# A fused attention and spectral kernel on one core: a room for each transposed tile, full-width score units, and a new order

## The chip, the cores and the metric

The kernel runs on one core of a Trainium2 chip. A core has five engines that run their own instruction streams: TensorE (PE) for matrix products, VectorE (DVE), ScalarE (ACT) and GpSimd (POOL) for elementwise work, and SyncE (SP), which here only issues transfers. Matrix products read SBUF and write PSUM, eight banks of 128 partitions x 2 KB. Engines wait for each other on semaphores. The metric is device microseconds of one execution. Before the change three runs took 235.37 us in the median (235.24 to 236.7).

## The reference

Two branches over the same 2048 x 640 input are mixed by a gate. Branch A is attention of 32 heads of 20 columns in four segments of 512 tokens: causal softmax inside a segment, and a linear memory over the segments before.

```
for s in range(4):
    p = softmax(q[s] @ k[s].T * scale + causal mask)
    a_dot = p @ v[s]
    a_mem = (phi(q[s]) @ M) / (phi(q[s]) @ z + 1e-6)     # phi(t) = t+1 if t>0 else exp(t)
    o[s] = g * a_mem + (1 - g) * a_dot                   # g = sigmoid(beta), by head
    M += phi(k[s]).T @ v[s];  z += phi(k[s]).sum()
a = o @ wo
b = irfft2(rfft2(x) * (w_r + 1j * w_i))
out = gate * a + (1 - gate) * b                          # gate = sigmoid(x . gate_w), by token
```

## The kernel before

**One recorded list, one order.** `Kern.record` (L866) does not issue anything: it records operations in a list, each with the buffers that it reads and writes. `Sched.schedule` (L117) then takes the constant `ORDER`, a list of some 2,300 numbers; each names an operation and the engine that does it, where two can. This order was made beforehand and is written into the file. So each engine's instruction stream is fixed, and each stream runs in order. `Sched.emit` puts in the semaphore waits. A transfer waits in SP's stream like an instruction in another, so what stands behind it on SP waits too.

**Modes of PE.** Most products use the full array (mode 0). Scores contract over 20 rows and run in four row tiles (mode 1). Products with few output partitions run in four column tiles of 32 (mode 2); a product of 128 output columns may be split into four of them when the neighbours in the order are column-tiled. `FLAT` in `finish_tile` names one output tile that is kept in mode 0.

**Attention.** Per segment the projections of queries and keys (`proj`) go to PSUM, to SBUF, to a scratch tensor in DRAM, and back as padded tiles `qkp` (L602). Eight groups of four heads follow, two to a pair. `qk_unit` (L1326) makes one unit of scores into the four banks of the pool "qk", which holds one unit at a time, and one exponential (L1367, in the last segment L1358) takes them to `ex` in SBUF. Keys come in pieces of kinds a, b and c. Kinds a and b are a full unit of 2048 columns for one group; kind c has 512 columns per group. `wide(s)` says whether kind c is done for four groups at once, a full unit for two pairs (segments 1 and 2), or for two, half a unit for each pair (segments 0 and 3). `masks` (L1373) lets POOL zero the upper triangle of the diagonal blocks and copy half blocks into place (L1404). In segments 0 to 2 the product with the values is made transposed (`pv_flipped`), stored to a scratch tensor and loaded again as `oU` for the output projection; in segment 3 it is made directly (`pv_group`) and transposed on PE at the end (`last_transposes`).

**The last segment's own layout.** Segment 3 keeps its exponentials with a pitch of 1280 columns per head, in three rooms of 5120 columns which lie across the rooms of the segments before. Therefore exponentials of its first three groups are recorded behind the last readers of several older rooms (`ex3`). Kind b there takes two exponentials (1280 and 768 columns) per group, and kind c two of 512 per pair.

**Memory.** `mem_read` reads the memory of the segments before; for segments 1 and 2 its result goes to a scratch tensor `o_scr`, and `finish_tile` (L1629) loads it back transposed as `mT`, 128 tokens a time, and adds it to `oU` (L1657). There are eight such loads (L600) and three rooms for them, taken in turn; these rooms lie in the space that the transform's tables use before. Each load also waits for its room.

**Transform.** `fft` makes column and row transforms as matrix products (`F1`, `D`, `T`), the product with the filter on DVE (L1560), and the inverse (`Tb`, `Db`) into `G`, which `finish_tile` reads. The operands `eo` of the last step lie on `xT[0]`.

**Output.** `finish_tile` adds the gated transform (`Fb`) and the output projection (`oproj`, helper L565 for products that were split into column tiles, L567 for others) in PSUM; ACT or DVE evicts (`ot`) and SP stores.

Of the kernel before, what the change touches and what calls it, by code (L numbers as in the profile page):

```python
# [7 lines left out]
ACT = mybir.ActivationFunctionType  # L8
# [502 lines left out]
class Kern:  # L511
# [84 lines left out]
    def dma(self, dst, src, nbytes, r, w, prio, tr=False, name="", after=(), queue="sp"):  # L596
# [1133 lines left out]
```

## Time and profile before

| what | value |
|---|---|
| median of three runs | 235.37 us (235.24 to 236.7) |
| the profiled execution, its own time | 237.45 us |
| its span, first to last instruction | 235.7 us |
| PE, DVE, ACT, POOL busy | 95%, 83%, 82%, 64% |
| granted TensorE clock | 0.993 |
| matmuls in the trace | 4377 of 4391 |
| transfers | 42.19 MB, mean 179 GB/s |

The tables of the profile group instructions by line, engine and operands: out<-in with shapes, the count, busy time and mean duration in ns of one, then the idle time of that engine in front of them and what ended it. "PEld" is the loading of weights, which overlaps matmuls. A row of the timeline has start, length, engine and group. Most matmuls are recorded by one helper line (L567) and evictions by another (L577 on ACT, L579 on DVE), so the tile names tell them apart. Since matmuls are pipelined, the distance from one start to the next tells more than the duration of one.

### The profile page before, as it was taken

What the parts mean: (1) busy time and instruction counts of PE and PEld (TensorE: products, weight loads), DVE (VectorE), ACT (ScalarE), POOL (GpSimd) and SP (SyncE); (2) the same over time, 40 slices, a digit from 0 to 9 for tenths busy, and PEclk for the clock granted to TensorE, in tenths of its full rate; (3) what the DMA queues carried; (4) which work ended last, traced back from release to release, by engine and by line L of the source; (5) the groups of instructions that cost most, each with busy time, mean ns of one, the idle gap of its engine ahead of it and who ended that gap; (6) DMA issues with size and microseconds to landing.
All of it is one profiled execution on the core that took longest, in us unless ns stands there. A gap on an engine that the chain in (4) does not pass through costs nothing.

```text
span 235.7 us, 10361 instructions
## 1 busy us (share of the span) xinstructions
PE 224.1 (95%) x4377; PEld 141.7 (60%) x4391; DVE 195.1 (83%) x497; ACT 193.1 (82%) x221; POOL 151.0 (64%) x299
## 2 busy tenths in 40 slices
PE   6799999999999999999999999999999999999993
PEld 2477577666546666555556645656544467667793
DVE  0169998799999996899999898999899984856563
ACT  2069997989899999999999889999999789787720
POOL 8233128445766886566786558677879687797810
PEclk9799999999999999999999999999999999999999
DMA  6999959999989356978654686376969687463124
GB/s 150 280 340 245 238 146 167 175 212 200 192 234 219 85 164 192 215 161 208 181 157 128 196 239 204 106 214 210 215 168 275 207 147 127 114 107 109 37 83 113
DMA packets 59266, 42.19 MB, mean 179 GB/s; under 512 B 30228, under 2 KB 55380, under 8 KB 59220
## 3 DMA queue, kind: packets, MB, share of 16 engines
q1 hardware_dynamic: 58180, 40.96, 73.8%
q8 instruction: 34, 0.56, 1.0%
q10 hardware_dynamic: 1040, 0.57, 0.9%
q14 instruction: 12, 0.10, 0.1%
HBM read 23.32 MB, written 12.30 MB: 151 GB/s over the span
## 4 chain that ended last, share of the span: by engine, by line
PE 71%; DVE 17%; DMA 7%; issue 2%; ACT 1%; SPq 1%; DVEq 0%
PE psum L567 63%; PE psum L565 8%; DVE Pt L1560 3%; DMA qkp<-qk_scr 3%; DMA xT<-in_A_x_dram 2%; DMA Wt<-in_B_w_r_dram 2%; DVE va L1183 2%; DVE G L1606 1%; DVE ub L579 1%; DVE Cp L579 1%; DVE mem L1228 1%; DVE dn L1223 1%; DVE mem L1225 1%; DVE qu L579 1%; ACT ex L1358 1%
## 5 line engine op out<-in xcount | busy, mean ns | idle before, releaser
L1404 POOL TENSOR_SCALAR_AFFINE_SELECT ex<-ex 128x256 bf16<-128x256 bf16 (+3 forms) x224 | 104.7, 487 | 40.1 <-ACT ex L1367 6.2
L1367 ACT ACTIVATE ex<-psum 128x2048 bf16<-128x2048 f32 (+1 forms) x56 | 101.7, 1816 | 7.9 <-PE psum L567 6.3
L1358 ACT ACTIVATE ex<-psum 128x1280 bf16<-128x1280 f32 (+3 forms) x32 | 36.2, 1130 | 7.4 <-PE psum L567 6.7
L567 PE MATMUL psum<-qkp 20*64 20x64 bf16 (+5 forms) x1280 | 32.1, 270 | 1.6 <-ACT ex L1367 1.0
L567 PE MATMUL psum<-xT,wk 128*128 128x256 bf16 (+1 forms) x280 | 33.0, 286 | 0.2
L567 PE MATMUL psum<-xT,wq 128*128 128x512 bf16 (+1 forms) x121 | 29.1, 422 | 2.9 <-DMA xT<-in_A_x_dram 2.1
L567 PE MATMUL psum<-wv,xT 128*32 128x321 bf16 (+3 forms) x385 | 26.8, 301 | 0.0
L1560 DVE TENSOR_TENSOR Pt<-psum,Wt 128x642 bf16<-128x642 f32 x32 | 25.5, 821 | 0.4
L567 PEld LDWEIGHTS psum<-xT,wk 128*128 128x128 bf16 (+1 forms) x280 | 20.4, 102 | 7.7 <-issue 3.0
L567 PEld LDWEIGHTS psum<-qkp 20*64 20x64 bf16 x1280 | 13.5, 103 | 18.0 <-ACT ex L1367 10.3
L973 POOL TENSOR_TENSOR xsb<-xf 128x320 bf16<-128x320 bf16 (+2 forms) x11 | 8.1, 743 | 19.8 <-DVE xf L968 10.5
L565 PE MATMUL psum<-wo,oU 128*32 128x320 bf16 x460 | 19.9, 300 | 0.0
L567 PE MATMUL psum<-big,Cp 128*128 128x321 bf16 (+1 forms) x96 | 19.1, 303 | 0.2
L567 PE MATMUL psum<-big,Ac 128*128 128x160 bf16 (+2 forms) x96 | 18.1, 257 | 0.3 <-DVE va L1183 0.2
L579 DVE CAST ot<-psum 128x320 bf16<-128x320 f32 x21 | 9.9, 489 | 9.3 <-PE psum L565 6.9
L567 PEld LDWEIGHTS psum<-wv,xT 128*32 128x32 bf16 (+1 forms) x385 | 13.4, 96 | 7.0 <-issue 1.8
L567 PE MATMUL psum<-ex,va 128*32 128x64 bf16 (+3 forms) x576 | 17.2, 256 | 0.3 <-ACT qu L577 0.3
L1183 DVE TENSOR_TENSOR va<-psum,ebx 128x320 bf16<-128x320 f32 x32 | 15.3, 485 | 2.0 <-PE psum L567 0.7
L567 PE MATMUL psum<-tt,Yt 128*128 128x256 bf16 (+1 forms) x96 | 16.2, 275 | 0.4 <-ACT qu L577 0.2
L1606 DVE TENSOR_TENSOR G<-eo,psum 128x320 bf16<-128x320 f32 x32 | 14.7, 478 | 2.1 <-PE psum L567 1.9
L567 PEld LDWEIGHTS psum<-ex,va 128*32 128x32 bf16 x576 | 10.9, 96 | 8.6 <-issue 1.3
L1140 ACT ACTIVATE et<-qu 128x512 bf16<-128x512 bf16 x25 | 15.6, 626 | 0.0
(103 smaller groups left out, 405.2 us busy)
## 6 DMA issues: line engine op xcount, KB each, us to landing
qkp<-qk_scr SPq DMA_DIRECT2D x28, 160.0 KB
tt<-tab_tt SPq DMA_DIRECT2D x8, 512.0 KB, 4.2
qk_scr<-qu SPq DMA_DIRECT2D x12, 256.0 KB, 3.8
u_scr<-ub SPq DMA_DIRECT2D x12, 256.0 KB, 3.6
xsb<-in_A_x_dram SPq DMA_DIRECT2D x8, 320.0 KB, 5.7
oU<-u_scr SPq DMA_DIRECT2D x15, 128.0 KB, 4.9
out_dram<-ot SPq DMA_DIRECT2D x12, 160.0 KB
Wt<-in_B_w_r_dram SPq DMA_DIRECT2D x16, 80.2 KB, 3.6
```

The lines of the kernel that those rows point to most:

```text
L565: h = e.matmul(dst, wt, r_, start=st, stop=sp_, **{**kw, "tile_position": (0, q), "skip_group_check": True})
L567: h = e.matmul(o_, l_, r_, start=st, stop=sp_, **kw)
L579: alts["dve"] = (lambda e: e.tensor_copy(dst(), src()), 67 + 1.04 * n, 68.0)
L973: self.either(lambda e, dst=dst, src=src, d0=d0, n=n, op=op: e.tensor_tensor(xs.ap(o + dst, [D, 2], [1, n]), xf.ap(src + d0, [321, 2], [1, ...
L1140: self.one("act", lambda e: e.activation(et.ap(0, [1, L]), qsl(), ACT.Exp), L, [qb], [b("et", pi_)], late, fix=95, name="phi_exp")
L1183: self.one("dve", lambda e: e.tensor_tensor(va.ap(i * H * VW + h0 * VW, [VW, nh], [1, DH]), self.ps(bank, 0, [DH, nh], [1, DH]), self.ebx. ...
L1223: self.one("dve", lambda e: e.reciprocal(dn.ap(16, [1, 16]), dn.ap(0, [1, 16])), 16, [db], [rb], prio, fix=145, name="mem_rec")
L1358: self.one("act", lambda e, d=d, q=q: e.activation(self.ex.ap(*d), self.ps(bank, *q), ACT.Exp, scale=SC), (2048, (1280, 768)[x], 512)[kind ...
L1367: self.one("act", lambda e, d=d, q=q: e.activation(self.ex.ap(*d), self.ps(bank, *q), ACT.Exp, scale=SC), 2048 if kind < 2 else 512 * n, [ ...
L1404: self.one("pool", lambda e: e.affine_select(self.ex.ap(*d, p0=p0, np_=np_), self.ex.ap(*q, p0=p0, np_=np_), [[0, 4], [1, n]], ALU.is_ge, ...
L1560: self.one("dve", lambda e, ri=ri, Pt=Pt, Wt=Wt, wo_=wo_, bank=bank: e.tensor_tensor(Pt.ap(ri * 322, [644, 2], [1, KD]), self.ps(bank, 0, ...
L1606: self.one("dve", lambda e, q=q, n2=n2, bank=bank, eo=eo: e.tensor_tensor(self.G.ap(n2 * D + 639 * q, [1 - 2 * q, 320]), eo.ap(q, [1, 320] ...
```

## The change

Three things are changed by hand and one follows from them.

1. **Rooms for the memory tiles.** Each of the eight `mT` tiles has a room of its own. Three of segment 2 keep the old rooms; the fourth lies on `qu[0]`, the four of segment 1 on `xT[0]`, which is free after the projections of segment 2. So that `xT[0]` is free, `eo` moves to `phk`, and one slice of the output weights from `phk` to `et`.
2. **Full-width score units.** Segment 3 uses the layout of the other segments (pitch 1088, kind c apart), so kind b is one exponential of 2048 columns. Kind c is done for four groups at once in segment 3 and in the second half of segment 0. The half blocks that segment 3 needs side by side are copied by the masks into a new room `X2COL`, on `Macc` (free after the last memory update); kind c of groups 4 to 7 lies on `ub`.
3. **Recording.** `fft_out` is split off `fft` and recorded after all segments. `FLAT` names another tile.
4. **A new `ORDER`** for all engines: 100 lines of numbers, nearly all different. Where an operation can go to two engines the choice may differ as well.

```
-        self.mT = [TL(f"mT{i}", [P, 5 * P]) for i in range(3)]
+        self.mT = {(2, i + 1): TL(f"mT{i}", [P, 5 * P]) for i in range(3)}
...
-        self.eo = [T(f"eo{i}", [P, 322], F32, at=self.xT[0].off + i * 1344) for i in range(3)]
+        self.mT.update({(1, i): T(f"mTx{i}", [P, 5 * P], at=self.xT[0].off + i * 1280) for i in range(4)})
+        self.mT[2, 0] = T("mTq", [P, 5 * P], at=self.qu[0].off)
...
+        self.eo = [T(f"eo{i}", [P, 322], F32, at=self.phk[0].off + i * 1344) for i in range(3)]
...
-            if self.wide(s):
+            if self.wide(s, pr):
...
-    def wide(self, s):
-        return s in (1, 2)
+    def wide(self, s, pr):
+        return s > 0 or pr > 1
...
     def exo(self, s, g):
-        return g % 3 * 5120 if s == 3 else self.EBASE + ((s * 8 + g) % 3) * 4 * self.EPITCH
+        return self.EBASE + ((s * 8 + g) % 3) * 4 * self.EPITCH
...
-        if s == 3:
-            step = self.exo(s, g + 1) - e0 if kind == 2 else 0
-            if kind == 0:
-                outs = [((e0, [1280, 4], [1, 512]), (0, [512, 4], [1, 512]))]
-            elif kind == 1:
-                outs = [((e0 + 576, [1280, 4], [1, 320]), (0, [512, 4], [1, 320])), ((e0 + 960, [1280, 4], [1, 192]), (320, [512, 4], [1, 192]))]
-            else:
-                outs = [((e0 + 896 + x * step, [1280, 4], [320, 2], [1, 64]), (x * 128, [512, 4], [64, 2], [1, 64])) for x in range(2)]
...
+        if kind == 2:
+            d, q = (self.exc(s, g), [128, 4], [512, n], [1, 128]), (0, [512, 4], [128, n], [1, 128])
         else:
...
+            d, q = (e0 + 576 * kind, [self.EPITCH, 4], [1, 512]), (0, [512, 4], [1, 512])
...
+                self.mask(s, g, P, (x0 + 64, cp), (e0 + 896, ep), 64, ("b0",), ("x2",), prio, 64)
+        elif s == 3:
+            self.mask(s, g, P, (x0, cp), (c0, cp), 64, ("c0",), ("x2c",), prio, 0)
+            self.mask(s, g, 64, (c0, cp), None, 64, (), ("c0",), prio, 0, 64)
+            self.mask(s, g, 64, (c0, cp), None, P, (), ("c0",), prio, -64)
...
-    FLAT = ((1, 0, 1),)
+    FLAT = ((1, 2, 0),)
...
-                self.mtc = getattr(self, "mtc", -1) + 1
-                k3 = self.mtc % 3
-                mT, mb = self.mT[k3], b("mT", k3)
+                mT, mb = self.mT[s, a], b("mT", s, a)
+                if s == 1:
+                    home = [b("xT", 0, c) for c in range(5)]
+                else:
+                    home = self.after_mid(("mT", a)) if a else [b("qu", 0, x) for x in range(2)]
```

On PE the same 4391 matmuls stand in a new order. ACT has 213 instructions for 230, DVE 499 for 497, POOL 303 and SP 239 on both sides.

More of the change, by code (lines that the diff above doesn't have):

```diff
@@ L808, in alloc @@
         self.va = [T(f"va{i}", [P, 4 * H * VW + 16]) for i in range(2)]
-        self.wo = [T(f"wo{c}", [P, D], at=self.pkn.off + 1280 * c if c < 4 else self.phk[0].off) for c in range(5)]
+        self.wo = [T(f"wo{c}", [P, D], at=self.pkn.off + 1280 * c if c < 4 else self.et[0].off) for c in range(5)]
         self.oU += [T("oU1", [P, 5 * L], at=self.phq.off), T("oU2", [P, 5 * L], at=self.va[0].off)]
         self.NEX = 3
-        self.ex = T("ex", [P, self.ONCOL + 4 * D])
+        self.ex = T("ex", [P, self.X2COL + 3 * 4 * P])
         self.cur = self.ex.off + 2 * self.ONCOL
@@ L822, in alloc @@
         self.Macc = T("Macc", [P, 880], F32)
+        assert self.ub[0].off == self.ex.off + 2 * self.UBCOL and self.Macc.off == self.ex.off + 2 * self.X2COL
         self.Mz = [T(f"Mz{i}", [P, 880]) for i in range(2)]
@@ L926, in late_weights @@
         for c in range(5):
-            home = [b("pkn", t) for t in range(5)] if c < 4 else [b("phk", k, x * L) for k in range(2) for x in range(2)]
+            home = [b("pkn", t) for t in range(5)] if c < 4 else [b("et", k) for k in range(2)]
             self.dma(lambda c=c: self.wo[c].ap(0, [1, D]), lambda c=c: dap(self.wo_d, 4 * c * D, [DH * D, H], [D, 4], [1, D]),
@@ L1300 @@
     ONCOL = MBASE + 512
+    UBCOL = ONCOL + 2 * 4 * D
+    X2COL = UBCOL + 4 * L + 4 * P
     def exb(self, s, g, k):
-        if s == 3:
-            return self.b("ex3", g % 3, k)
+        if s == 3 and (k[0] == "x" or k == "c0" and g > 3):
+            return self.b("ex3", g % 3 if k[0] == "x" else g, k)
         if k == "c0":
@@ L1307, in exb @@
         return self.b("ex", (s * 8 + g) % 3, k)
[L1309 to L1312 removed]
     def exo(self, s, g):
[L1315 removed]
+        return self.EBASE + ((s * 8 + g) % 3) * 4 * self.EPITCH
     def exc(self, s, g):
[L1318 removed]
+        return 512 * g if g < 4 else (self.UBCOL if s == 3 else self.MBASE + 768) + 512 * (g - 4)
     def exm(self, s, g):
@@ L1323, in exall @@
     def exall(self, s, g):
-        return [self.exb(s, g, k) for k in ("a0", "b0", "c0", "m1", "m3") + ("b1",) * (s == 3)]
+        return [self.exb(s, g, k) for k in ("a0", "b0", "c0", "m1") + (("m3",) if s < 3 else ("x2", "x2c"))]
     def qk_unit(self, s, pr, u, unit):
@@ L1348, in qk_unit @@
         e0, n = self.exo(s, g), len(gps)
-        if s == 3:
-            step = self.exo(s, g + 1) - e0 if kind == 2 else 0
-            if kind == 0:
-                outs = [((e0, [1280, 4], [1, 512]), (0, [512, 4], [1, 512]))]
-            elif kind == 1:
-                outs = [((e0 + 576, [1280, 4], [1, 320]), (0, [512, 4], [1, 320])), ((e0 + 960, [1280, 4], [1, 192]), (320, [512, 4], [1, 192]))]
-            else:
-                outs = [((e0 + 896 + x * step, [1280, 4], [320, 2], [1, 64]), (x * 128, [512, 4], [64, 2], [1, 64])) for x in range(2)]
-            for x, (d, q) in enumerate(outs):
-                self.one("act", lambda e, d=d, q=q: e.activation(self.ex.ap(*d), self.ps(bank, *q), ACT.Exp, scale=SC), (2048, (1280, 768)[x], 512)[kind], [bank],
-                         [self.exb(s, 2 * pr + (x if kind == 2 else gp), ks + str(x * (kind == 1))) for gp in gps], prio - self.QK_LEAD, name="exp" + str(x)[x == 0:],
-                         after=[q for gp in gps if 2 * pr + gp < 3 for q in self.ex3(2 * pr + gp)])
-        else:
-            if kind == 2:
-                d, q = (self.exc(s, g), [128, 4], [512, n], [1, 128]), (0, [512, 4], [128, n], [1, 128])
-            else:
-                d, q = (e0 + 576 * kind, [self.EPITCH, 4], [1, 512]), (0, [512, 4], [1, 512])
-            home = [b("xf", k) for k in range(3)] if s == 0 and kind == 2 and pr > 1 else []
-            self.one("act", lambda e, d=d, q=q: e.activation(self.ex.ap(*d), self.ps(bank, *q), ACT.Exp, scale=SC), 2048 if kind < 2 else 512 * n, [bank],
-                     [self.exb(s, 2 * pr + gp, ks + "0") for gp in gps], prio - self.QK_LEAD, name="exp", after=home)
@@ new lines, in qk_unit @@
+        if kind == 2:
+            d, q = (self.exc(s, g), [128, 4], [512, n], [1, 128]), (0, [512, 4], [128, n], [1, 128])
+        else:
+            d, q = (e0 + 576 * kind, [self.EPITCH, 4], [1, 512]), (0, [512, 4], [1, 512])
+        home = [b("xf", k) for k in range(3)] if s == 0 and kind == 2 and pr > 1 else []
+        if s == 3 and kind == 2 and pr > 1:
+            home = [b("ub", k, x) for k in range(2) for x in range(2)]
+        self.one("act", lambda e, d=d, q=q: e.activation(self.ex.ap(*d), self.ps(bank, *q), ACT.Exp, scale=SC), 2048 if kind < 2 else 512 * n, [bank],
+                 [self.exb(s, 2 * pr + gp, ks + "0") for gp in gps], prio - self.QK_LEAD, name="exp", after=home)
@@ L1405, in mask @@
             self.ex.ap(*d, p0=p0, np_=np_), self.ex.ap(*q, p0=p0, np_=np_), [[0, 4], [1, n]], ALU.is_ge, 0.0, base=base, channel_multiplier=-1), 4 * n,
-            [self.exb(s, g, k) for k in rk], [self.exb(s, g, k) for k in wk], prio, per=0.793, fix=218, name="mask")
+            [self.exb(s, g, k) for k in rk], [self.exb(s, g, k) for k in wk], prio, per=0.793, fix=218, name="mask",
+                 after=[self.b("Macc", t) for t in range(5)] * (wk[0][0] == "x"))
         self.Sc.ops[-1].part = p0 > 0
@@ L1435, in pv_group @@
                         items.append((th, 22))
-                self.mms(items, [self.exb(s, g, k) for k in (("a0",), ("a0", "b0", "m1"), ("a0", "b0", "b1", "c0", "m1"), ("a0", "b0", "b1", "c0", "m1", "m3"))[i]] + [b("va", s % 2, jj) for jj in range(i + 1)] + [bank], [],
+                self.mms(items, [self.exb(s, g, k) for k in (("a0",), ("a0", "b0", "m1"), ("a0", "b0", "m1", "x2", "x2c"), ("a0", "b0", "c0", "m1"))[i]] + [b("va", s % 2, jj) for jj in range(i + 1)] + [bank], [],
                          prio, name="pv")
@@ L1585, in fft, with fft_out @@
                            after=[b("xsb", q) for q in range(8)])
+    def fft_out(self):
+        b = self.b
+        tot = 10.3 + 65.7 + 51.3
+        tf = lambda c: self.F_START + (self.F_END - self.F_START) * c / tot
+        big = self.big
+        acb = [b("Ac", c, nb) for c in range(5) for nb in range(4)]
         cpb = [b("Cp", g, c0) for g in range(16) for c0 in (0, 2)]
@@ L1602, in fft @@
                     self.Sc.op(self.copy_alts(lambda eo=eo: eo.ap(0, [1, KD]), lambda bank=bank: self.ps(bank, 0, [1, KD]), KD),
-                               r=[bank], w=[eb], prio=prio, name="ev_Db", after=[b("xT", 0, c) for c in range(5)])
+                               r=[bank], w=[eb], prio=prio, name="ev_Db", after=[b("phk", x, y * L) for x in range(2) for y in range(2)])
                     continue
```

45 lines of the change are left out of this document (16 added, 29 removed), and 188 rows, old and new, of the table ORDER.

## The prediction

> **What bounds the kernel now.** I read the busy shares of the whole span first:
>
> ```profile
> PE 224.1 (95%) x4377; PEld 141.7 (60%) x4391; DVE 195.1 (83%) x497; ACT 193.1 (82%) x221; POOL 151.0 (64%) x299
> ```
>
> That line is one average. The second view is the busy time in three stretches: the middle (attention over segments 0 to 2 beside the transform), the tail (the last segment beside the output projections), and the finish.
>
> ```profile
> 45.00:185.00 140.00, 135.84 (x2454) 81.23 (x2463) 130.93 (x333) 130.33 (x138) 99.92 (x207) 1.00 0.79 192
> 185.00:229.00 44.00, 43.89 (x1274) 31.26 (x1270) 30.52 (x79) 32.84 (x39) 30.93 (x57) 1.00 0.51 109
> 229.00:236.00 7.00, 2.98 (x88) 2.62 (x80) 2.77 (x6) 0.44 (x1) 0.00 (x0) 1.00 0.36 98
> ```
>
> The columns are length, PE, PE's weight loads, DVE, ACT, POOL, clock, DMA. In the tail PE is busy 43.89 of 44.00 us, while ACT and DVE have 11 and 13 us free. So there only less PE work shortens the time. In the middle PE is not busy for 140.00 - 135.84 = 4.16 us, ACT (130.33) and DVE (130.93) are busy 93% too, and the three wait for each other in turn. The third view, the waits of the weight loads in the same 140 us, says on whom:
>
> ```profile
> PEld psum L567 <- ACT ex L1367: 10.1, 35, 0.9
> ```
>
> Weight loads waited 35 times for an exponential: all four score banks are one room, so the next score unit starts only when the exponential has read the last one. Most of these 10.1 us pass beside matmuls still running. The order of the first 30 us hardly changes. Neither does the finish: behind the last matmuls
>
> ```profile
> 230.31 1.67 PE L567 MATMUL psum<-wo,oTl 128*32 128x320 bf16 x44
> ```
>
> come a copy and the store on both sides, some 3.7 us to the span's 235.7. What can move is the middle and the tail.
>
> **The change, part by part.**
>
> **Changes of tile mode on PE.** The number of matmuls is 4391 on both sides, of the same shapes. What differs is how often PE goes between full-array, row-tiled (scores) and column-tiled work. In the program's order I count 211 such changes before and 204 after: 167 and 166 up to the first output projection, 44 and 38 behind it. What one costs, from start to start:
>
> ```profile
> 138.76 0.30 PE L567 MATMUL psum<-wv,xT 128*128 128x320 bf16 x1
> 138.99 0.73 PE L567 MATMUL psum<-ex,va 128*32 128x512 bf16 x24
> 139.54 1.02 PE L567 MATMUL psum<-wv,xT 128*32 128x320 bf16 x24
> 140.49 0.43 PE L567 MATMUL psum<-qkp 20*64 20x512 bf16 x12
> 140.97 0.31 PE L567 MATMUL psum<-wv,xT 128*128 128x321 bf16 x1
> 141.11 0.30 PE L567 MATMUL psum<-big,Ac 128*128 128x321 bf16 x1
> 219.54 0.31 PE L565 MATMUL psum<-wo,oU 128*32 128x320 bf16 x4
> 219.68 0.31 PE L567 MATMUL psum<-G,fbg 128*32 128x320 bf16 x4
> ```
>
> Without a change a 321-column matmul takes 141.11 - 140.97 = 0.14 us of PE, and four column-tiled ones of 320 take 219.68 - 219.54 = 0.14. With one, the 320 columns at 138.76 take 0.23: 0.09 for the change. The 24 tiled ones at 139.54 take 0.95 where six fours need 0.84: 0.11. Seven fewer at 0.11 are **-0.8 us**; six of them lie in the tail, where nothing can absorb the gain. Ends: 0.09 each gives -0.6, and double that, -1.3, if those that vanish also hid a wait.
>
> **Cover of the waits.** This is the large term, and an estimate. For each group of matmuls that reads what ACT, DVE or POOL made, I went back in the program's order to the matmul that this came from, and set the PE work that stands in between (columns at 0.14 us for 321, plus the changes of mode) against the durations of the instructions on the way. For a score unit the way is the exponential of the unit before:
>
> ```profile
> L1367 ACT ACTIVATE ex<-psum 128x2048 bf16<-128x2048 f32 x52 | 97.6, 1877 | 7.4 <-PE psum L567 6.0
> L1367 ACT ACTIVATE ex<-psum 128x1024 bf16<-128x1024 f32 x4 | 4.1, 1023 | 0.5 <-PE psum L567 0.3
> L1358 ACT ACTIVATE ex<-psum 128x2048 bf16<-128x2048 f32 x8 | 15.0, 1877 | 3.8 <-PE psum L567 3.8
> L1358 ACT ACTIVATE ex<-psum 128x1280 bf16<-128x1280 f32 x8 | 9.9, 1237 | 2.1 <-PE psum L567 2.0
> L1358 ACT ACTIVATE ex<-psum 128x768 bf16<-128x768 f32 x8 | 6.5, 810 | 0.3
> L1358 ACT ACTIVATE ex<-psum 128x512 bf16<-128x512 f32 x8 | 4.8, 597 | 1.2 <-PE psum L567 0.9
> L1560 DVE TENSOR_TENSOR Pt<-psum,Wt 128x642 bf16<-128x642 f32 x32 | 25.5, 821 | 0.4
> ```
>
> So fewer than about 2.1 us of PE work between two score units (1.877 and a hand-over) means a wait that no luck removes; behind the product with the filter (L1560) it is 0.82 and a hand-over. Before, 26 groups of the middle lack 4.8 us in all, 10 of them score units; in the tail none lacks any. That agrees with the 4.16 and 0.11 us in which PE is not busy, and so I trust the count. After, 18 groups of the middle lack 2.3 us (8 are score units), and 2 of the tail lack 0.56 (a score unit and one that follows the transform's last sums). The difference is -2.5 + 0.56 = -1.9 us. The count knows nothing of ACT and DVE being held up by other work in their own queues, and both are 93% busy; so I take **-1.4**, with 0 and -1.9 as the ends.
>
> **The exponentials themselves.** Before they take 52 x 1.877 + 4 x 1.023 + 8 x (1.877 + 1.237 + 0.810 + 0.597) = 137.9 us; after, 71 of 2048 and 2 of 1024 columns take 135.3: 2.6 us and 17 instructions less, and 73 score units for 76. Of the 2.6 nearly all is in the last segment, the tail, where ACT has 11 us to spare: its worth is in the cover above, and **0** by itself.
>
> **Copies that change engines.** Net, two 512-wide evictions go from ACT to DVE; from POOL to DVE go one sum with the memory tile, one normalisation, one gate table and one sum of the last segment, and one transform sum goes to POOL.
>
> ```profile
> L579 DVE CAST qu<-psum 128x512 bf16<-128x512 f32 x16 | 11.0, 685 | 1.9 <-PE psum L567 1.4 <-ACT et L1140 0.3
> L1657 DVE TENSOR_TENSOR oU<-oU,mT 128x640 bf16<-128x640 bf16 x6 | 3.2, 550 | 0.5 <-DMA mT<-o_scr 0.5
> L1649 DVE TENSOR_TENSOR oU<-oU,r 128x512 bf16<-128x512 bf16 x10 | 3.7, 418 | 0.0
> L1090 DVE TENSOR_TENSOR fbg<-fcat,gbc 128x512 bf16<-128x512 bf16 x2 | 1.4, 683 | 0.0
> L1450 DVE TENSOR_TENSOR on<-on,mem 128x320 bf16<-128x320 bf16 x4 | 1.6, 426 | 0.0
> L1565 DVE TENSOR_TENSOR Yt<-Pt 128x321 bf16<-128x321 bf16 x17 | 5.2, 322 | 0.0
> ```
>
> DVE gets 2 x 0.685 + 0.550 + 0.418 + 0.683 + 0.426 - 0.322 = 3.1 us more. The four from POOL are work for the output and lie mostly in the tail, where DVE has 13 us free: **0**. The two evictions (1.4 us) can fall in the middle; without cover they cost +1.4, and as they free ACT as much, as little as -1.4. I take 0.
>
> **Masks.** Eight of 128x256 go and eight of 64x256 come:
>
> ```profile
> L1404 POOL TENSOR_SCALAR_AFFINE_SELECT ex<-ex 128x256 bf16<-128x256 bf16 x104 | 42.7, 421 | 16.2 <-ACT ex L1367 2.7 <-DVE oU L1649 2.1 <-DVE Ac L579 1.8
> L1404 POOL TENSOR_SCALAR_AFFINE_SELECT ex<-ex 64x256 bf16<-64x256 bf16 x48 | 19.9, 416 | 12.3 <-DVE phk L1153 5.1 <-PE psum L567 2.0 <-DVE phq L1153 1.7
> ```
>
> At 421 and 416 ns these are equal: 0. The layout of the last segment is now that of the others, so its first units no longer wait for several old rooms at once; that is in the cover too.
>
> **The rooms for the memory tiles.** The only wait on such a load stands in the L1657 row above: 0.5 us of DVE, in a tail where PE is never idle. So having them early is worth **0**, 0.5 at most. But the loads are on SP's queue:
>
> ```profile
> L600 SPq DMA_TRANSPOSE mT<-o_scr x8: 1227/1293/1911, 167.8 to 206.9; - x8
> DMA to landing us min/median/max: 4.5/4.5/4.5
> ```
>
> Before, three of the eight stand ahead of the last load of padded queries and keys on that queue; after, seven do, four more. Each holds the queue for 1.29 us, and the score units wait for what stands behind it. I take 0, as the projections run far ahead of their scores in both orders; the other end is 4 x 1.29 = +5.2.
>
> **Sum.** -0.8 - 1.4 = -2.2 us. The profiled execution took 237.45 us (span 235.7), 2.1 more than the median of the runs, 235.37. From 237.45 the sum gives 235.25; applied to the median, **233.2 us**, 0.9% less. A measurement of this kernel can tell about 1%, 2.4 us, from no change.
>
> **The rivals.** *More than the count says.* The 10.1 us of weight loads behind exponentials are mostly hidden below "busy", as matmuls are pipelined. If the new order takes the share from them that it takes from my count (2.5 of 4.8, a half), that is -5.0, with the modes and the tail's 0.56 about -5.3: 230.1 us. For it: the weight loads are busy 58% of the middle and 71% of the tail, so the middle has more slack than PE's 97% shows. Against it: a hidden wait costs nothing where the next group had work to overlap. [...]
>
> *Nothing is gained.* ACT and DVE set the pace of the middle through their own queues, the 3.1 us more on DVE eat the cover, and the six changes of mode in the tail are paid back by its two new waits (0.56): about 235.2 us. For it: both at 93%.
>
> *Slower: the transposes hold up the padded loads.* One place decides: a load of queries and keys behind a transpose lands after PE has come to its score unit. The chain of waits shows that such loads can be last:
>
> ```profile
> 39.78 6.37 DMA qkp<-qk_scr
> 150.37 4.47 DMA Wt<-in_B_w_r_dram
> ```
>
> If all four count, +5.2, with the modes and the tail's 0.56 net +5.0: 240.3 us. From two of them on (+2.6, net +2.4), the result is over 1% slower. Against it stands a row of SP's own waits,
>
> ```profile
> SPq L602 <- PE psum L567: 23.0, 12, 5.2
> ```
>
> 23 us in which the queue had nothing to issue, so it isn't full. [...]
>
> That the change doesn't do what it says is excluded by the program's order: the eight loads go to eight rooms.
>
> **How the numbers follow.** The forecast has 0.55, with a range of its own from 232.2 to 234.5; more gain 0.12; nothing 0.18; slower 0.15. About two fifths of the forecast's own case lie below 233.0, so faster by over 1% has 0.22 + 0.12 = 0.35 rounded up; slower by over 1% is 0.15, all of its rival but a little, and some from DVE's +1.4; within 1% the rest, 0.50. The range goes from 230.9, most of the way to the full 230.1, to 237.7, two of the four transposes, and leaves out somewhat under 2 in 10.
>
> **What would show it.** Right: in the middle PE is not busy for about 2.5 to 3 us instead of 4.16, the wait of weight loads for exponentials falls clearly below 10.1, and the tail, from the first output projection to the last matmul, is 0.5 us shorter at the same fullness. Wrong: waits of score units for padded loads, a DVE above 94% in the middle with PE waiting for it, or a tail with gaps of a microsecond.

## The result and the profile after

The changed kernel took **239.36 us** (median of 13 runs, 237.75 to 242.68) where the kernel before, run beside it, took 236.7 us (13 runs). The ratio, over the executions within 1.5% of the fastest of their kernel, is **1.0102**, with a 95% interval of 1.0068 to 1.0136: slower by 1.0%, where 0.9% faster was forecast. Applied to the 235.37 us that the prediction starts from, this gives 237.8 us; 233.2 was forecast, and 237.7 was the upper end of the range. The profiled execution of the changed kernel took 241.51 us, span 239.7 us, above the median, so its profile is good for telling where the time sits, less good for its size.

The busy times of the kernel after, over the whole span:

```profile
PE 225.8 (94%) x4391; PEld 142.5 (59%) x4391; DVE 195.9 (82%) x499; ACT 189.5 (79%) x204; POOL 148.1 (62%) x299
```

And in the middle and the tail (length, then PE, PE's weight loads, DVE, ACT, POOL, clock, DMA):

```profile
45.00:185.00 140.00, 133.72 (x2369) 79.90 (x2368) 126.34 (x321) 124.68 (x128) 96.59 (x204) 0.99 0.80 186
185.00:229.00 44.00, 42.09 (x1168) 28.92 (x1169) 31.34 (x82) 33.22 (x28) 28.63 (x56) 1.00 0.41 113
```

ACT is 3.6 us less busy, as the exponentials and evictions promised, and DVE 0.8 more. But PE is not busy for 140.00 - 133.72 = 6.28 us of the middle, not 4.16 or the forecast 2.5 to 3, and for 1.91 us of the tail, not 0.11. On whom PE's matmuls wait (total us, times, longest; the longest rows), first before, then after:

```profile
PE psum L567 <- DMA xT<-in_A_x_dram: 2.1, 1, 2.1
PE psum L567 <- DVE G L858: 1.3, 1, 1.3
PE psum L567 <- ACT ex L1367: 1.0, 3, 0.5
PE psum L567 <- ACT qu L577: 0.4, 2, 0.3
```

```profile
PE psum L567 <- issue: 2.5, 2, 1.8
PE psum L567 <- DMA tt<-tab_tt: 2.1, 2, 1.2
PE psum L567 <- DVE G L861: 1.3, 1, 1.3
PE psum L567 <- DVE eo L579: 1.1, 1, 1.1
PE psum L567 <- DMA xT<-in_A_x_dram: 1.0, 1, 1.0
PE psum L567 <- ACT ex L1357: 0.9, 4, 0.3
```

Three waits are new, in five pieces: 5.7 us ("issue" alone had 0.2 before). The wait for x at the start is 1.1 us shorter in this profile; in four profiles of the changed kernel it is 1.0 to 2.0 us, so I put that down to the execution and not to the change. The chain of waits of the kernel after (start, length, what) shows two of them and what stands behind the third:

```profile
47.35 1.84 issue
128.33 1.65 PE psum L567 x43
129.98 5.67 DMA tt<-tab_tt
135.78 4.03 PE psum L567 x74
139.81 6.75 DMA tt<-tab_tt
180.58 6.99 DMA oU<-u_scr
187.59 0.43 DVE oU L1645
188.02 0.40 DVE eo L579
```

So the chain goes from transfers to PE. Both table loads start at the moment when matmuls end (128.33 + 1.65 = 129.98 us, and 139.81 us): those matmuls read the old tile, and their end releases its room. The table tile `tt` (512 KB, the transform's tables) and a block of `oU` arrive late; the latter stops DVE's division at L1645, and the eviction of `eo` that PE needs stands behind it in DVE's queue. The time of a table load from issue to landing, before and after:

```profile
DMA to landing us min/median/max: 3.3/4.2/4.2
```

```profile
DMA to landing us min/median/max: 3.7/5.3/6.7
```

"Issue" is a wait for nothing that the profile shows by name. Here it stands inside one group of equal matmuls (timeline of the kernel after: start, length, group, idle time before it):

```profile
46.64 0.71 PE L567 MATMUL psum<-wv,xT 128*32 128x320 bf16 x13
49.19 0.32 PE L567 MATMUL psum<-wv,xT 128*32 128x321 bf16 x3 [1.84 <-issue]
```

Some 1.5 us behind this gap PE ran at half of its clock for 3.5 us (length, PE busy, granted clock, DMA share, GB/s):

```profile
50.70:54.20 3.50, 3.50 (x21) 0.51 0.31 78
```

The page of the kernel after lists a DMA queue that carries instructions (packets, MB, share of 16 engines):

```profile
q8 instruction: 34, 0.56, 1.0%
```

These are 34 packets of 0.56 MB / 34 = 16 KB. The page names no engine for them. In the mean PE begins 251 matmuls and weight loads from one packet to the next (125 to 355; 250 in the kernel before, 138 to 379), and so I take them for PE's instructions; that is an estimate. In the trace one of them starts at 46.40 us and takes 1.33 us; by then PE has begun 1398 matmuls and weight loads, where the packet at this place in the kernel before starts at number 1324. Over all 20 profiles the gap behind this packet grows with that number: none up to 1324 (seven profiles), 0.5 us at 1340, 0.9 to 1.2 us from 1356 to 1372, 1.5 to 1.8 us from 1380 to 1438. So I read the wait of 1.84 us as PE having run out of instructions. That too is my estimate, from these counts; no view names what PE waited for.

### The profile page after: what moved, and what is told of

It is laid out like the page before. It is cut to its first block, busy times and chain, and to the rows that moved or that the text cites. A ratio compares the mean times of both kernels' runs of the same rounds, so it can differ in the third digit from the quotient of the medians.

```text
span 239.7 us, 10358 instructions
## 1 busy us (share of the span) xinstructions
PE 225.8 (94%) x4391; PEld 142.5 (59%) x4391; DVE 195.9 (82%) x499; ACT 189.5 (79%) x204; POOL 148.1 (62%) x299
## 4 chain that ended last, share of the span: by engine, by line
PE 66%; DMA 12%; ACT 10%; DVE 6%; issue 3%; SPq 2%; ACTq 0%
PE psum L567 59%; ACT ex L1357 7%; PE psum L565 7%; DMA tt<-tab_tt 5%; DMA oU<-u_scr 3%; DMA qkp<-qk_scr 2%; DMA xT<-in_A_x_dram 2%; SPq L602 1%; DVE Pt L1548 1%; ACT et L1144 1%; ACT qu L577 1%; SPq L600 1%; DVE Cp L579 1%; DVE mem L1229 1%; DVE G L1602 1%
## 5 line engine op out<-in xcount | busy, mean ns | idle before, releaser
L1357 ACT ACTIVATE ex<-psum 128x2048 bf16<-128x2048 f32 (+1 forms) x73 | 135.3, 1854 | 16.5 <-PE psum L567 15.2
L567 PE MATMUL psum<-xT,wq 128*128 128x512 bf16 (+1 forms) x135 | 31.7, 380 | 1.0 <-DMA xT<-in_A_x_dram 1.0
L567 PE MATMUL psum<-wv,xT 128*32 128x321 bf16 (+3 forms) x385 | 27.8, 303 | 1.9 <-issue 1.8
L567 PEld LDWEIGHTS psum<-wv,xT 128*32 128x32 bf16 (+1 forms) x385 | 13.8, 97 | 10.1 <-issue 3.6
L579 DVE CAST ot<-psum 128x320 bf16<-128x320 f32 x22 | 10.4, 488 | 9.9 <-PE psum L565 7.5
L567 PE MATMUL psum<-big,Cp 128*128 128x321 bf16 (+1 forms) x96 | 17.2, 302 | 0.3 <-DVE G L1602 0.2
L567 PE MATMUL psum<-tt,Yt 128*128 128x256 bf16 (+1 forms) x96 | 16.8, 276 | 0.3
L567 PE MATMUL psum<-big,Ac 128*128 128x160 bf16 (+2 forms) x96 | 16.7, 260 | 0.0
L567 PE MATMUL psum<-Bt,tt 128*128 128x321 bf16 x64 | 13.9, 302 | 2.1 <-DMA tt<-tab_tt 2.1
```

Of the source, the lines that this page charges most:

```text
L567: h = e.matmul(o_, l_, r_, start=st, stop=sp_, **kw)
L579: alts["dve"] = (lambda e: e.tensor_copy(dst(), src()), 67 + 1.04 * n, 68.0)
L1357: self.one("act", lambda e, d=d, q=q: e.activation(self.ex.ap(*d), self.ps(bank, *q), ACT.Exp, scale=SC), 2048 if kind < 2 else 512 * n, [ ...
```

## The experiments

**First: the transposes or the order.** The *transposes' theory* is the slower rival of the prediction: four more transposed loads ahead of the last padded loads. The *order's theory* says that the loss comes with the new order of the engines, whatever the rooms do. Four kernels ran beside one kernel before. The changed kernel again:

> The changed kernel as it is, for a profile of an undisturbed execution (the one at hand took 241.51 us where most take 237.75 to 239.8). Both theories expect 1.005 to 1.015 of the kernel before. The transposes' theory (early loads of the memory tiles hold up the table loads on SP and the DMA engines) expects PE to wait some 2 us for table tiles again, around 130 to 148 us; the order's theory (PE, ACT and DVE meet worse in the new order) expects the loss spread over score units and evictions. The 1.8 us in which PE waited for nothing visible at 47 us, followed by a half-clock window, is expected to be gone if it was that execution's alone, and to come back if the order makes it.

Measured: ratio 1.0245 (1.0154 to 1.0336), above what both theories expected; waits for tt 2.9 us, eo 2.2, issue 1.8, and 0.9 for the transposed keys `pkn`. The first three are the places of the first profile. None of the four is a padded load, and the loss is not spread over score units either.

The changed kernel with segment 1's four transposes late on SP's queue, as before (`ORDER`; 4068, 4384, 4286 and 4188 are the four loads):

```
-        1252, 4068, 1330,
+        1252, 1330,
...
-        4012, 3748,
+        4012, 4188, 4068, 3748,
...
-        3178, 3464,
+        3178, 4286, 4384, 3464,
```

> The changed kernel, with only the four transposed loads of segment 1 put back behind the table loads on SP (two at about 170 us, two behind the last padded load); all else in the new order. The transposes' theory expects 1.5 to 2.5 us less than the changed kernel, 0.998 to 1.004 of the kernel before, and no wait of PE for table tiles. The order's theory expects no difference from the changed kernel (1.010 +- 0.004).

Measured: 1.038 (1.0283 to 1.0477): not faster, as the transposes' theory had it, and rather slower, though the interval overlaps the one above. One wait for tt is gone (1.0 us once, not 2.9), but eo grew:

```profile
PE psum L567 <- DVE eo L579: 3.3, 1, 3.3
PE psum L567 <- DMA xT<-in_A_x_dram: 1.7, 1, 1.7
PE psum L567 <- issue: 1.5, 2, 1.1
```

The transposes' theory misses its number. But this test moves the trouble too: two of the late transposes (174.0 us, 3.41 us) now stand among the loads of `oU`, and DVE waits 3.13 us for such a load, which holds up eo. The next pair, in the old order, is the cleaner test.

The kernel before with the rooms alone (part 1 of the diff and `fft_out`, one slice of `wo` loaded later as its room is another), and the same with the four transposes early, in three cases right behind a table load:

```
+        self.mT.update({(1, i): T(f"mTx{i}", [P, 5 * P], at=self.xT[0].off + i * 1280) for i in range(4)})
...
-        1450, 1363,
+        1450, 4322, 1363,
```

> The kernel before with only the new rooms (eight memory tiles, operands of the last transform step and one weight slice moved) and the old order, but for that weight slice, which is loaded later. Nothing is loaded earlier. Both theories expect 1.000 +- 0.004 of the kernel before.

> The same as the one with the rooms alone, but the four transposed loads of segment 1 stand early on SP, three of them right behind a table load, as in the changed kernel. The transposes' theory expects 1 to 2.5 us more than the rooms alone, 1.004 to 1.011 of the kernel before, with PE waiting for tables or padded loads. The order's theory expects 1.000 +- 0.004.

Measured: 1.0182 (1.0063 to 1.0302) and 1.0123 (1.0046 to 1.02), both above what either theory expected. The first profile loses 3.8 us to issue in two pieces near 198 and 205 us; the second has 2.0 us of waits for padded loads at 37 to 47 us, where nothing differs from the kernel before. That could be the spread of executions, so the second kernel ran once more at the end:

> The kernel before with the rooms and the early transposed loads alone, once more in more executions. If the rooms cost by themselves: ratio 1.006 to 1.02 again, and the profile shows where: a wait of PE behind 100 us that the kernel before lacks. If the first result was the spread of executions (its profile's extra waits, 2.0 us for qkp, stand at 37 to 47 us, where nothing differs from the kernel before): ratio 0.997 to 1.006.

Measured: **1.0044** (1.0008 to 1.008), 12 runs. The rooms and the early loads cost 0.1 to 0.8%; most of the first 1.2% was spread. On the same chip the changed kernel gave 1.0154 to 1.0336 above, so most of its loss there has another cause. With the old order, early transposes are worth little, which speaks against the transposes' theory. The kernel with the rooms and late transposes was not run again, and its 1.8% stays open.

**Second: mending late arrivals on SP's queue.** The *arrivals theory*: PE waits for a few single transfers, and one refill of instructions, which the new order leaves too little time. The *coupling theory*: ACT, DVE and PE wait for each other, and the transfers are only where it shows. One transposed load of x behind the load of `hm` (2310), three blocks of `oU` earlier (4012, 4004, 4008), and other transfers out of the way of the table loads (3974 a slice of `wo`, 2264 and 2786 stores of memory sums, 3100 a store of queries and keys). The changed kernel did not run beside these four, so their ratios can only be set against its 1.0102 to 1.0245 in other comparisons. From the second piece of code on, only the places that the transfers go to are shown:

```
-        606, 2310, 1864,
+        606, 1864,
...
+        62, 2310, 529,
```

> The changed kernel with one DMA moved: the one-block transposed load of x that SP issues at 43.5 us goes behind the load of hm, where the kernel before has it. Arrivals theory (what the change lost, it lost because single transfers and one refill of PE's instructions come later than the new order needs them): the refill of PE's instructions (packets of the instruction queue) at 46.4 us begins earlier, counted in PE instructions (about 1340 instead of 1419 to 1459), PE's wait called issue at 47 to 49 us (1.8 to 2.1 us) goes, and the total falls by 1 to 2 us, to a ratio of 1.005 to 1.015 against the kernel before. Coupling theory (ACT, DVE and PE wait for each other in the new order, and the transfers are only where that shows): the wait goes to another name within the next 10 us and the total stays within 0.5 us of the changed kernel's 243.5 on this kind of chip, 239.4 over all.

Measured: 1.0283 (1.0236 to 1.033). Issue at 47 us is 0.9 instead of 1.8, but exponentials cost 2.8 us instead of 0.9.

```
-        3996, 3712,
+        3996, 4012, 4004, 4008, 3712,
```

> The changed kernel with three loads moved: blocks 2, 3 and 4 of segment 0's output from u_scr to oU, which the changed kernel issues between 167 and 175 us, go right behind block 0, some 5 to 10 us earlier (their room has been free since about 160 us). Arrivals theory: DVE's division of oU (L1645) no longer waits for its load at 180 to 188 us, so the eviction to eo behind it on DVE is in time, and PE's wait for eo (1.1 to 3.3 us in the three profiles) falls below 0.3; total 1 to 2 us less. Coupling theory: PE waits at 180 to 190 us as long, for ACT or DVE under another name; total unchanged.

Measured: 1.0276 (1.0235 to 1.0318). The wait for eo is gone, as the arrivals theory said; the total is not under what the changed kernel gave elsewhere:

```profile
PE psum L567 <- DMA pkn<-phk: 2.9, 2, 1.5
PE psum L567 <- DMA tt<-tab_tt: 2.6, 2, 1.5
PE psum L567 <- issue: 2.3, 6, 1.0
PE psum L567 <- DVE G L1602: 1.7, 3, 1.2
```

```
-        2438, 3070,
+        2438, 3974, 3070,
...
-        1446, 1355,
+        1446, 2264, 1355,
...
-        1532, 1592,
+        1532, 3100, 2786, 1592,
```

> The changed kernel with four DMAs moved out of the way of the last three 512 KB table loads: a slice of wo goes 6 us earlier, and two stores of memory sums and one store of queries and keys go behind the table load that they stood ahead of. The table loads themselves start where their room becomes free, as in both kernels. Arrivals theory: their time from issue to landing falls from a median of 5.3 to 5.5 us towards the 4.2 of the kernel before, PE's two waits for a table tile (2.1 to 2.9 us) fall below 1, total 1 to 2 us less. If the room's release decides and not the queue (a variant of the arrivals theory), landing falls but PE still waits 1 us or more. Coupling theory: waits change their name, total unchanged.

> All three at once, except that the transposed load of x goes 4 places earlier instead of later (issued about 40.8 us). Arrivals theory: the three savings add to 3 to 5 us, which brings the kernel to the level of the kernel before or under it, ratio 0.99 to 1.003, and PE's busy share to 95 to 96%. Coupling theory: ratio 1.01 or more, as for the changed kernel.

Measured: 1.0185 (1.0133 to 1.0237) and 1.02 (1.0159 to 1.024), 0.8 to 1% under the two runs beside them. That is a hint for the arrivals theory, unless the moves in those two cost something by themselves. No wait is put down to tt in either profile, though the median time of a table load to landing stays at 5.2 and 5.1 us and does not fall towards 4.2. But both wait 1.3 us for an eviction to `qu`, which itself waits for a store (the tile `qu` in the last kernel: what DVE's instructions on it waited for):

```profile
  DMA qk_scr<-qu: 1.3, 1
```

That store is one that I had moved behind a table load: the mend made a wait of its own.

**Third: what one late arrival costs in the kernel before, and which half of the order.** The changed kernel again; its code with the kernel before's order for the first 1100 and the first 680 of 2311 operations (`head`; renumbered, and one slice of `wo` loaded later), then its own (the files hold the numbers themselves; the first piece of code says it in short); and the kernel before with one table load (1450) issued later:

```
-    ORDER = after
+    ORDER = before[:head] + [x for x in after if x not in before[:head]]
```

```
-        3040, 1450, 1363,
+        3040, 1363,
...
-        1538, 3490,
+        1538, 1450, 3490,
```

> The changed kernel itself once more, for a comparison on one chip with the three runs beside it. Both theories: ratio 1.01 to 1.025, PE's waits for issue at 47 to 49 us (about 1.8), for a table tile (1 to 3 us in one or two waits) and for eo (1 to 2 us).

> The changed kernel's code (rooms and units) with the order of the kernel before on all engines for the first 1100 of 2311 scheduled operations (up to about 110 us), and the changed kernel's order from there on. Arrivals theory: the refill of PE's instructions at 47 us and the transposed load of keys at 78 us are in time again, so that issue falls from 1.8 to under 0.5 and the 1 us for pkn goes; the waits for table tiles and eo behind 110 us stay; the seam itself costs up to 2 us, as what the new order had done earlier is caught up on there. Ratio 1.005 to 1.02, at or a little under the changed kernel's. If the losses of the changed kernel lay in the last segment's full-width units, they would all be here as well, and the ratio would not fall under the changed kernel's.

> The same with the seam at operation 680 (about 65 us): only the first quarter has the order of the kernel before. Arrivals theory: the wait called issue at 47 us goes (1.8 us), the waits for pkn, table tiles and eo stay; ratio 0.005 to 0.01 under the changed kernel's, 1.005 to 1.015. Coupling theory: the middle is the same as in the changed kernel from 70 us on, and so is the ratio.

> The kernel before with one DMA moved: the seventh 512 KB table load is issued some 6 us later, so that it lands about when PE comes to it, as in the changed kernel. It prices one such late arrival. Arrivals theory: PE waits 0.5 to 2 us for tt once, and the total rises by that or more (if a window of half clock follows the gap, 1.7 us more): ratio 1.003 to 1.015. Coupling theory: the middle of the kernel before has slack between ACT, DVE and PE, a late tile is caught up on within the next units, ratio within 0.003 of 1.

Measured: 1.0154 (1.0083 to 1.0224), 1.0186 (1.0139 to 1.0232), 1.015 (1.0089 to 1.021). With the old first quarter the stall near 47 us falls from 1.7 to 0.5 us, and issue is 0.3 us in all with the old first half, yet the total is that of the changed kernel; the half's seam cost waits of its own (2.4 us for exponentials, 1.4 for `qu`). So either the first half isn't where the loss is, or the seam eats what it saves; these two don't tell. The last kernel gave **1.0071** (1.0039 to 1.0102): one transfer issued 4 us later (at 140.92 instead of 137.00 us in the two traces) costs 0.0071 x 237 = 1.7 us. PE's timeline there:

```profile
145.01 0.45 PE L567 MATMUL psum<-Bt,tt 128*128 128x321 bf16 x2 [1.62 <-DMA tt<-tab_tt]
```

The total rises by about the wait (by 0.9 to 2.4 us, going by the interval); the coupling theory had expected it to be absorbed. Half clock is not needed for it: of the executions that this comparison rests on, those with a clock above 0.993 have a median span of 236.6 us, against 235.2 of the kernel before.

**Fourth: mends by PE's order, and all mends.** The changed kernel again; then two groups of matmuls that read a table tile first (1424 with 1428, and 1510) later on PE alone; then these with the moves on SP except the harmful store and the load of x, and a load of the filter (1018) behind `hm`; last, that with one block of `oU` moved and not three, and the products on `pkn` (2288, 2290) one unit later:

```
-        2210, 1424, 2254,
+        2210, 2254,
...
+        2256, 1424, 1428, 1430,
...
-        2798, 1510, 2974,
+        2798, 2974,
...
+        1442, 1510, 2826,
```

```
+        62, 1018, 529,
...
+        740, 2288, 2290, 2364,
```

> The changed kernel once more, as the measure for the two mends beside it on the same chip. Ratio 1.01 to 1.025 by what it gave so far.

> The changed kernel with three groups of matmuls moved back in PE's order: the two that read the sixth table tile first go behind the next 48-matmul product of the scores with the values (0.8 us of PE work), the one that reads the seventh first goes behind two groups of the transform (0.7 us). Nothing moves on SP's queue. Arrivals theory: the waits for tt (1 to 3 us in the profiles of the changed kernel) shrink by about 0.7 each, to 0 to 1.5 us in all, and the total by 0.7 to 1.5 us, or 0.003 to 0.006 of the ratio. Coupling theory: ACT and DVE, one unit later, take it back; ratio as the changed kernel's beside it, within 0.003.

> All mends without the harmful one: PE's order as in the run before, the slice of wo 6 us earlier, the two stores of memory sums behind the table loads that they stood ahead of, the blocks of oU earlier, and one 80 KB load of the filter behind the load of hm instead of ahead of the refill of PE's instructions. Arrivals theory: no wait for tt or eo above 0.5 us, a total of 2 to 4 us less than the changed kernel beside it, ratio 1.0 to 1.01; it would equal the kernel before only if the refill came in time too. Coupling theory: ratio 1.01 or more, with the 2 to 3 us of named waits gone but spread over other waits.

> The changed kernel with PE's order mended for the table tiles as before, the slice of wo and two stores of memory sums out of their way, one 80 KB load of the filter behind the load of hm, one block of oU (not three) 4 us earlier, and the two matmul groups that read the transposed keys of segment 0's second half moved behind the next score unit (1.2 us later). Arrivals theory: no wait for tt, pkn or eo above 0.5 us; left are issue at 47 us (1 to 1.8) and what both kernels have; undisturbed executions at 236 to 237.5 us of span instead of 237.7 to 238.4, ratio 1.002 to 1.012. Coupling theory: ratio 1.013 or more, with other waits in place of those mended.

Measured: 1.0181 (1.0121 to 1.0241), 1.0163 (1.0097 to 1.0229), 1.0196 (1.0129 to 1.0263); the last, on another chip, 1.0214 (1.0136 to 1.0292). Named waits fell: tt from 2.4 to 1.5 us in the second, tt and eo to nothing in the third, where `pkn` (1.9 us), issue (1.8) and a wait for G (1.1) are left. The fourth:

```profile
PE psum L567 <- issue: 1.3, 2, 1.0
PE psum L567 <- ACT ex L1357: 1.2, 5, 0.3
PE psum L567 <- DVE qu L579: 1.0, 1, 1.0
PE psum L567 <- DMA tt<-tab_tt: 0.9, 2, 0.6
PE psum L567 <- DMA pkn<-phk: 0.7, 1, 0.7
```

No mend brought the ratio below the interval of the changed kernel beside it (1.0121 to 1.0241; beside the fourth it did not run). The second lies 0.2% below it and the third 0.2% above it, each uncertain by some 0.9% or 2 us. That is too coarse for the 0.7 to 1.5 us that the arrivals theory expected of the second; of the 2 to 4 us that it expected of the third, it leaves the lower end at most. The theory is right on the waits for tt and eo and wrong on the sum: other waits are there when these are mended. That is what the coupling theory expected of the total.

**Fifth: one late block of `oU` in the kernel before** (4092 behind the load of the last denominators):

```
-        3650, 4092, 1720,
+        3650, 1720,
...
-        3246, 1776,
+        3246, 4092, 1776,
```

> The kernel before with one DMA moved: a block of segment 1's output (u_scr to oU) is issued some 4 us later, behind the last denominators' load, so that DVE's division waits for it and holds up what is behind it on DVE. It makes the chain transfer, DVE, PE that the changed kernel has at 180 to 188 us. Arrivals theory: PE waits 1 to 2 us for a DVE eviction at 184 to 190 us and the ratio is 1.004 to 1.01 from that alone; if half-clock stretches come with such gaps, more of its executions than one in five (the kernel before: 10 of 46) have a granted clock of 0.993 or less, and those are 1 to 1.7 us longer. Coupling theory: absorbed, ratio under 1.003.

Measured: **1.0187** (1.0111 to 1.0263), as much as the changed kernel, and more than the 1.004 to 1.01 that the arrivals theory expected. DVE's timeline shows the division that waits:

```profile
188.38 0.76 DVE L1650 TENSOR_TENSOR oU<-oU,r 128x512 bf16<-128x512 bf16 x2 [3.06 <-DMA oU<-u_scr]
```

PE's waits show what comes of it:

```profile
PE psum L567 <- DVE G L1607: 2.2, 1, 2.2
```

And PE in stretches around it (length, PE busy, granted clock, DMA share, GB/s):

```profile
187.40:189.60 2.20, 0.01 (x1) 1.00 0.80 220
189.60:191.70 2.10, 1.91 (x36) 1.00 0.81 210
191.70:198.50 6.80, 6.80 (x118) 0.50 0.47 115
198.50:205.00 6.50, 6.50 (x180) 1.00 0.53 79
```

One transfer issued at 185.7 instead of 179.2 us (in the two traces) stops DVE for 3.06 us and PE for 2.20; 2 us behind the gap PE's clock is halved for 6.8 us, in which it does 118 matmuls where the next 6.5 us have 180. PE is "busy" all the time, so no view of waits shows this half of the price: at half clock 6.8 us lose up to 3.4. Four of the six executions of this kernel have a granted clock of 0.983 or less, and two of the eleven of the kernel before beside it.

## Why the prediction was wrong

**Changes of mode, -0.8 us: not seen.** Two profiles at full clock that hold all 4391 matmuls have PE busy for 224.7 us (the rooms and early loads, the old order) and 225.3 us (the last mend, nearly the new order; 206 changes of mode by its trace, against 211): no gain in PE's busy time. Whether it was there and was hidden in other differences is open.

**Cover of the waits, -1.4 us: the step that failed.** The count went from each group of matmuls back to what ACT, DVE or POOL had to do for it. It had no term for groups that read what a transfer brings, nor for the waits called issue, the longest of which I read as a late refill of PE's own instructions; both were put at nothing without a reason. In the profile after, these waits are 5.7 us (issue 2.5, tt 2.1, eo behind a late `oU` 1.1). On what it counted it may have been right: without the 2.1 us for tt and the 1.8 for issue, the middle of the profile after has 6.28 - 3.9 = 2.4 us in which PE is not busy, near the 2.5 to 3 forecast, and the tail 1.91 - 1.1 (eo) - 0.7 (issue) = 0.1. But waits hide each other, and this subtraction isn't to be trusted: in the other three profiles of the changed kernel PE is not busy for 7.9, 7.9 and 9.4 us of the middle, and with the named arrivals down to 2.9 us (issue 1.3, tt 0.9, `pkn` 0.7) the last mend's middle still has 6.8 us:

```profile
45.00:185.00 140.00, 133.22 (x2410) 1.00 0.84 186
```

The sign that I had named, fewer weight loads waiting for exponentials, did not come either: 10.1 us in 34 waits, as before in 35 (45 to 185 us, after):

```profile
PEld psum L567 <- ACT ex L1357: 10.1, 34, 0.6
```

Nor is the tail shorter: from the first output projection to the last matmul it is 47.2 us before and 47.4 after. A sign of being wrong came, the gap of a microsecond: 1.1 us for eo, right ahead of the first output projection.

**Exponentials, 0, and copies, 0.** The exponentials take 135.3 us x73, as forecast, and ACT is 3.6 us less busy; that either is worth nothing by itself was not tested apart from the order. The step has a slip: of the 17 instructions fewer on ACT, 15 are exponentials (88 before, 73 after), and the other two are the evictions that go to DVE. DVE got 0.8 us, not 3.1.

**Rooms, 0 (up to +5.2): the size was about right, the mechanism not.** With the early loads and the old order they cost 0.4% (0.1 to 0.8%), some 1 us. That the transposes hold up padded loads is not borne out: PE's waits after name no padded load. The slower rival had the right sign by luck, and a wrong place. A rival on the table loads was missing: the two in the chain above are issued when PE releases their room, and PE is also who needs them next, so the new order of PE fixes both ends of their time, and the row "DMA to landing" of 4.2 us stood in the trace before.

**"The order of the first 30 us hardly changes"** was true (PE's weight loads come in the same order on both sides up to 41.7 us) and beside the point: the wait of 1.84 us called issue comes behind it, at 47 us.

**What stays open.** One late arrival is enough for 0.7% or 1.9% in the kernel before; that is shown. That these arrivals are the changed kernel's loss is supported by its profiles and not shown, as mending them did not bring the time back. The mends leave the order of PE, ACT and DVE as tight as it was, and each profile of a mended kernel names other waits. The changed kernel without the rooms, or the units without the new order, was not tried, so what the full-width units do by themselves is not known.

## What to carry to other kernels

When an order of work is made denser, list for each transfer the time from the release of its room to its first use, and set it against the measured time to landing of the same tile: a term that counts only engines says nothing on that. Price a wait of PE at more than its length, since a stretch of half clock can follow it; here 11 of the 21 gaps of 1.6 us or more had one behind them. And a wait that is mended is worth its length only when nothing else is due within it: here the waits for tt and eo went to nothing in one mend, and the ratio was 1.0196 beside 1.0181. Measure the sum, not the row.

## What the runs showed of the hardware

**Half clock follows gaps of PE.** In the 20 profiles PE has 81 gaps of 0.8 us or more (some perhaps for want of a record) and, ahead of the finish, 18 stretches of half clock, each 3.41 us long or two or three times that; 14 of the 18 begin within 2.5 us of the end of such a gap. Long gaps are the ones that are followed: 11 of the 21 of 1.6 us or more, and 3 of the 60 shorter ones. The other four stretches begin at 205 to 211 us with no such gap ahead of them, and what starts them is open. The kernel before has one, in its starved start, behind a gap of 2.1 us:

```profile
5.40:7.50 2.10, 0.04 (x1) 1.00 1.33 137
7.50:8.30 0.80, 0.76 (x20) 1.00 1.16 286
8.30:11.80 3.50, 3.50 (x56) 0.51 1.09 350
```

Of the executions that the comparisons rest on, 51 of 58 of the kernel before have a granted clock above 0.993, and 9 of 20 of the changed kernel. Those of the changed kernel have a median span of 237.1 us, the other eleven 239.8; the 51 of the kernel before have 235.2. So of the changed kernel's loss some 1.9 us are there at full clock, and some 2.7 more come in the executions with a half-clock stretch, longer gaps included. The gaps that were followed are 1.1 to 3.3 us long. What in a gap brings half clock on, and why other gaps of the same length have none behind them, no run here shows.

**Comparisons differ.** The same changed kernel gave 1.0102, 1.0245, 1.0154 and 1.0181 against the kernel before in four comparisons, the last three on different chips; two ratios that lie 1% apart say little unless they come from one comparison.
